# Router logits in two halves of 64 tokens, taken behind the values' products, and three smaller moves in a fused attention and expert kernel

## The chip, the core and the metric

The kernel is one launch on one core of a Trainium2 chip. The metric is the device time of that launch in microseconds (us), as the median of several runs. The profile names the engines: PE (TensorE, products), PEld (the loading of its weights, which overlaps PE), DVE (VectorE), ACT (ScalarE), POOL (GpSimd) and SP (SyncE, which here issues transfers).

## The reference, cut to what is computed

```python
def _attn_ref(q, k, v):                      # (4, 8, 576, 64) each
    scores = scale * np.matmul(q, k.transpose(0, 1, 3, 2))
    mask = (rel >= 0) & (rel < 64)           # a window of 64 keys
    ...
    attn = attn / (np.sum(attn, axis=-1, keepdims=True) + 1e-09)
    return np.matmul(attn, v)

def _moe_ref(x, w_gate, w_noise, noise, w1, w2):   # x (2304, 512), 8 experts, 1024 wide
    logits = x @ w_gate
    noise_scale = np.log1p(np.exp(x @ w_noise))
    noisy_logits = logits + noise_scale * noise
    top2 = np.argpartition(-noisy_logits, 2, axis=1)[:, :2]
    ...
    h = np.maximum(x[mask] @ w1[e], 0.0)
    out[mask] += top2_w[mask, k, None] * (h @ w2[e])

def _moe2_ref(x, w_in, w_out):               # 512 -> 2048 -> 512, a smooth gate between
    return g @ w_out
```

The output is `_moe2_ref(_moe_ref(_attn_ref(q, k, v)))`.

## The kernel before

**Stages.** The 2304 tokens are 18 tiles of 128. Attention and routing run first, up to about 103 us of the profile. Then the experts run in units: expert 0 as the units "0a" and "0b", experts 1 to 7, and last the wide layer. Everything is issued in the order in which the program writes it, engine by engine; no scheduler moves anything.

**The attention loop.** `step(u)` runs for u = 0 to 36, two steps for a tile. An even step u = 2m puts on PE, in this order: the masks and scores of tile m+1 (`A`, L355 and L364, products of 64 by 64), the turning of tile m-2's attention output (`Ex`, L422, four transposes), the turning of a block of probabilities (`C`, L387), and the values' products of tile m-1 (`Dm`, L401: 16 products, 32 on the chip since each fp32 product is two, with 64 weight columns; tokens 0 to 63 and 64 to 127 write different halves of the output partitions). The odd step has a second `C` and then the router's logits of tile m-2 (`Gm`, L440: four products with 128 weight columns and 16 moving columns, eight on the chip). Here one **turn** is the time from the `Ex` of one tile to the `Ex` of the next.

**The VectorE side of a turn.** Two reductions give the maxima of the scores (`top`, L371). `Dm` ends with the normalisation of tile m-1 (L406, L407, L409), which makes the tile `x` that the next turn's `Ex` reads. L443 copies the logits out of PSUM. Between them `advance` puts pieces of `route`, the routing of a group of tiles (8, 4 and 6 tiles): small operations on the logits and "marks", which are a row `ohr` by VectorE (L586) and a row `ohe` by VectorE (L593) or ScalarE (L596). `place` then gives each mark's product to PE (L634). When two groups are placed, `early` makes the first indexes and GpSimd gathers expert 0's rows.

**Banks.** The transposes of `C` and `Ex`, the logits and the routing counts take banks 3 and 5 in turn (`rot`). The values' products write the tile `OB`, two banks of which columns 0 to 259 are used. In unit "0b" (`WIDE - 1`) six blocks of the first full expert's rows are turned (`xpose`, L761): all in bank 7, and the sixth in bank 4. ScalarE copies each out (L767) and VectorE takes the difference (L768) before the next may write that bank.

**Loads.** SP loads keys and queries two tiles at a time (`load_qk`, L107 and L108), values, weights, and stores `x`.

## Time and profile before

| | us |
|---|---|
| median of 3 runs | 947.01 (946.17 to 947.58) |
| the profiled execution, whole | 950.02 |
| its span, first to last instruction | 948.3 |
| PE busy in the span | 935.7 |
| DVE, ACT, POOL busy | 665.6, 436.5, 186.2 |
| granted TensorE clock | 1.0 of full speed throughout |

PE is busy nearly all the time, but a pipelined engine that is shown busy need not be at its peak, and the share of busy time is a mean over stages. So the profile is read in stretches: busy time of each engine in each stretch, then the order of the instructions in a turn, then what ends the waits.

### The profile page before, as it was taken

The page shows a single profiled execution, that of the slowest core. Times are in us where ns is not written, and L with a number is a line of the kernel's source. Part 1 is how long each engine was busy: PE and PEld are TensorE (multiplying, and loading weights), DVE is VectorE, ACT ScalarE, POOL GpSimd, SP SyncE. Part 2 cuts the span into 40 slices and gives each one's busy share as a digit, 9 for nine tenths or more (in the row PEclk, how much of TensorE's full clock was granted, in tenths as well). Part 3 has the DMA queues.
Part 4 walks back from the last instruction along what each step waited for, and adds up shares of the span by engine and source line. Part 5 has one row for each costly group of instructions (what it writes and reads, how often), then busy time and mean ns, then how long its engine had stood idle before and what let it go on. Part 6 is the DMA issues. An engine that isn't in the chain of part 4 may idle for free. (4 is left out here: it accounts for less than half of the span.)

```text
span 948.3 us, 17990 instructions
## 1 busy us (share of the span) xinstructions
PE 935.7 (99%) x6779; PEld 832.3 (88%) x6781; DVE 665.6 (70%) x1411; ACT 436.5 (46%) x907; POOL 186.2 (20%) x249
## 2 busy tenths in 40 slices
PE   9999999999999999999999999999999999999998
PEld 6887888988888989898888889988999899899986
DVE  4689765477997968889533366767867776687664
ACT  6898314345565555555433266333433333342221
POOL 3222013133645353354402030000000000000000
PEclk9999999999999999999999999999999999999999
DMA  8874136555888878767725566775576559556521
GB/s 258 300 252 167 56 100 186 188 191 199 290 288 275 261 236 277 257 206 260 252 89 184 204 231 236 252 256 178 177 256 213 164 174 308 175 178 213 182 95 44
DMA packets 91274, 196.95 MB, mean 208 GB/s; under 512 B 7320, under 2 KB 18072, under 8 KB 91184
## 3 DMA queue, kind: packets, MB, share of 16 engines
q1 hardware_dynamic: 83152, 171.68, 54.6%
q0 software_dynamic: 6736, 21.86, 6.4%
q10 hardware_dynamic: 1296, 2.23, 0.6%
q8 instruction: 54, 0.88, 0.4%
q14 instruction: 36, 0.29, 0.1%
HBM read 155.45 MB, written 40.29 MB: 206 GB/s over the span
## 5 line engine op out<-in xcount | busy, mean ns | idle before, releaser
L969 PE MATMUL bank<-wo,hall 128*128 128x512 f32 x864 | 237.6, 394 | 0.0
L969 PE MATMUL bank<-w,hall 128*128 128x512 f32 (+3 forms) x944 | 234.6, 396 | 0.1
L969 PEld LDWEIGHTS bank<-w,hall 128*128 128x128 f32 (+3 forms) x944 | 167.7, 183 | 35.2 <-issue 0.3
L969 PEld LDWEIGHTS bank<-wo,hall 128*128 128x128 f32 x864 | 146.7, 188 | 17.4 <-DVE hall L915 0.2
L904 ACT ACTIVATE hall<-bank 128x288 fp32r<-128x288 f32 (+6 forms) x128 | 54.0, 422 | 218.4 <-PE bank L896 200.6
L896 PE MATMUL bank<-xhie,w 128*128 128x288 f32 (+4 forms) x768 | 122.5, 302 | 0.3 <-DVE hall L907 0.2
L896 PEld LDWEIGHTS bank<-xhie,w 128*128 128x128 f32 x768 | 113.5, 188 | 7.1 <-DVE hall L907 1.4
L907 DVE SCALAR_TENSOR_TENSOR hall<-bank,hall 128x288 fp32r<-128x288 f32 (+7 forms) x168 | 60.0, 391 | 82.5 <-ACT hall L904 75.1
L149 DVE TENSOR_TENSOR w<-raw,w 128x1024 fp32r<-128x1024 f32 (+1 forms) x69 | 81.9, 1188 | 23.8 <-ACT w L158 17.8
L1183 PEld LDWEIGHTS bank<-xb,wi 128*128 128x128 f32 x576 | 80.8, 188 | 8.4 <-DVE cg L1173 0.7
L1207 ACT ACTIVATE hall<-cg 128x512 fp32r<-128x512 f32 x64 | 40.3, 629 | 100.4 <-DVE cg L1205 100.4
L1183 PE MATMUL bank<-xb,wi 128*128 128x256 f32 x576 | 84.3, 282 | 0.3 <-DVE cg L1173 0.3
L1183 PEld LDWEIGHTS bank<-xc,wi 128*128 128x128 f32 x480 | 67.5, 188 | 6.5
L1183 PE MATMUL bank<-xc,wi 128*128 128x256 f32 x480 | 69.9, 280 | 0.0
L158 ACT ACTIVATE w<-raw 128x1024 fp32r<-128x1024 f32 (+1 forms) x71 | 69.4, 977 | 0.0
L896 PE MATMUL bank<-xloe,w 128*128 128x288 f32 (+4 forms) x384 | 69.0, 301 | 0.0
L1201 ACT ACTIVATE mg<-cg 128x512 f32<-128x512 f32 x64 | 40.1, 626 | 45.8 <-DVE cg L1173 44.1
L204 POOL TENSOR_TENSOR td<-rawd 128x512 f32<-128x512 f32 x32 | 33.3, 1040 | 139.6 <-DVE rawd L202 111.8
L896 PEld LDWEIGHTS bank<-xloe,w 128*128 128x128 f32 x384 | 58.0, 188 | 0.0
L1202 DVE SCALAR_TENSOR_TENSOR cg<-mg,cg 128x512 f32<-128x512 f32 x64 | 43.8, 684 | 18.8 <-ACT mg L1201 18.8
L1211 DVE SCALAR_TENSOR_TENSOR hall<-cg,hall 128x512 fp32r<-128x512 f32 x64 | 44.0, 687 | 8.1 <-ACT hall L1207 7.7
L1205 DVE SCALAR_TENSOR_TENSOR cg<-mg,cg 128x512 f32<-128x512 f32 x64 | 44.0, 687 | 1.0
(285 smaller groups left out, 1389.2 us busy)
## 6 DMA issues: line engine op xcount, KB each, us to landing
wi<-w1o SPq DMA_DIRECT2D x56, 1024.0 KB
raw<-wcat SPq DMA_DIRECT2D x64, 512.0 KB
rawd<-wd SPq DMA_DIRECT2D x32, 512.0 KB
w1o<-so SPq DMA_DIRECT2D x64, 256.0 KB
y<-y_dram SPq DMA_DIRECT2D x28, 256.0 KB
vE<-v SPq DMA_DIRECT2D x18, 260.0 KB
x_dram<-x SPq DMA_DIRECT2D x18, 256.0 KB
k<-kT SPq DMA_DIRECT2D x8, 512.0 KB
```

The lines of the kernel that those rows point to most:

```text
L149: nc.vector.tensor_tensor(out=w[:, 1, c], in0=t[:, c], in1=w[:, 0, c].bitcast(F32), op=ALU.subtract)
L158: nc.scalar.activation(w[:, 0, c], t[:, c], AF.Copy)
L896: nc.tensor.matmul(ps, lhsT=l[k], rhs=r[:, k, s:s + w], start=(c == 0), stop=(c == len(prods) - 1))
L904: nc.scalar.activation(hh, ps, AF.Relu)
L907: nc.vector.scalar_tensor_tensor(out=t, in0=ps[:, c], scalar=0.0, in1=hh[:, c].bitcast(F32), op0=ALU.max, op1=ALU.subtract)
L969: nc.tensor.matmul(M2[b][0:w], lhsT=h2[:, o:o + w], rhs=r[n], start=(first and a == 0), stop=(last and a == end))
L1183: nc.tensor.matmul(ps, lhsT=w[:, l, k * P:k * P + P], rhs=r[:, m, k, :], start=(c == 0), stop=(c == len(prods) - 1))
L1201: nc.scalar.activation(st["m"], c, AF.Relu, scale=0.5)
L1202: nc.vector.scalar_tensor_tensor(out=c, in0=st["m"], scalar=1.0, in1=c, op0=ALU.min, op1=ALU.subtract)
L1205: nc.vector.scalar_tensor_tensor(out=c, in0=st["m"], scalar=1.0, in1=c, op0=ALU.min, op1=ALU.mult)
L1207: nc.scalar.activation(h2[:, 0:T], c, AF.Copy, scale=-1.0)
L1211: nc.vector.scalar_tensor_tensor(out=h2[:, T:2 * T], in0=c, scalar=-1.0, in1=h2[:, 0:T].bitcast(F32), op0=ALU.mult, op1=ALU.subtract)
```

## The change

- **Logits.** `Gm` takes each 128-token tile as two halves of 64 tokens, so each product has 64 weight columns. It moves from the odd step to the even step, behind `Dm`, and writes columns 272 to 287 of `OB` in place of a bank of `rot`. `Dm` is now ahead of `early` and `advance`, and its normalisation is a function of its own, `norm`, that stays behind them.
- **Queries.** They are laid out tile by tile and half by half in DRAM, and loaded one tile at a time into four places.
- **Turned outputs.** For the first six tiles VectorE copies the turned output `xt`, between the two reductions; for the others ScalarE does, as before.
- **Banks.** The six transposes in unit "0b" take banks 7, 3, 5 and 4 in turn.

```diff
-    def load_qk(j):
-        q_t[j] = qbuf[:, j % 2]
+    def load_q(i):
+        nc.sync.dma_start(out=qbuf[:, i % 4], in_=qT[i])
+
+    def load_k(j):
         ...
             nc.sync.dma_start(out=kt[:, :, 64 + h.start:64 + h.stop], in_=kTv[:, :, t])
-            nc.sync.dma_start(out=q_t[j][:, :, h], in_=qTv[:, :, t])
+            if j < 2:
+                load_q(t.start // P)
+        if j == 1:
+            load_q(3)
...
+    def norm(u):
+        i, r = divmod(u, 2)
+        if r == 0:
+            return
         ov = OB[:, :, 0:4 * VW].rearrange("p b (h d) -> p b h d", d=VW)
...
-        nc.scalar.activation(xt.rearrange("p k t -> p (k t)"), XTb, AF.Copy)
         xts[i] = xt
+        if i < 6:
+            behind_top.append(lambda: nc.vector.tensor_copy(xt.rearrange("p k t -> p (k t)"), XTb))
+        else:
+            nc.scalar.activation(xt.rearrange("p k t -> p (k t)"), XTb, AF.Copy)
...
-        lg = (rot(u) if u <= NU else bank[0])[:, LGO:LGO + 2 * E]
+        lg = OB[:, i % 2, LGO:LGO + 2 * E]
         for k in range(4):
-            nc.tensor.matmul(lg, lhsT=xt[:, k, :], rhs=wg_sb[:, k, 0:2 * E], start=(k == 0), stop=(k == 3))
+            for h in (slice(0, 64), slice(64, P)):
+                nc.tensor.matmul(lg[h], lhsT=xt[:, k, h], rhs=wg_sb[:, k, 0:2 * E], start=(k == 0), stop=(k == 3))
...
             if (u + 2) % 4 == 0 and (u + 2) // 4 + 1 < NT // 2:
-                load_qk((u + 2) // 4 + 1)
+                load_k((u + 2) // 4 + 1)
                 keys_before((u + 2) // 4 + 1)
+            if u % 2 == 0 and u // 2 + 4 < NT:
+                load_q(u // 2 + 4)
...
             top(u + 2)
+            while behind_top:
+                behind_top.popleft()()
             top(u + 3)
         if u + 2 < NU:
             soft(u + 2)
 
-        if u % 2 == 1 and 0 <= m - 2 < NT:
+        place()
+        if 0 <= u - 1 < NU:
+            Dm(u - 1)
+        if u % 2 == 0 and 0 <= m - 2 < NT:
             logits(m - 2, u)
-        place()
         early()
         advance(MARKS[u > NU - 10])
         if 0 <= u - 1 < NU:
-            Dm(u - 1)
+            norm(u - 1)
...
     assert state["first"]
-    logits(NT - 2, NU)
     warm(2, Sb[0])
...
-                    prep_xpose(x, b, bank[0] if ui == WIDE else bank[4] if ui == WIDE - 1 and b == NB else TR)
+                    prep_xpose(x, b, bank[0] if ui == WIDE else bank[(7, 3, 5, 4)[b % 4]] if ui == WIDE - 1 else TR)
```

How the order moves at three places follows. In the rows `bank3_76` is bank 3 and so on, `p` are probabilities, `x13` is the output of tile 13, `xt13` the same turned.

PE before, in the turn of tile 13 (near 83 us of the profile), from the last values' product to the next masks:

```order
L401 MATMUL ob_106<-vE14_1429,pt29_1711 64x65
L387 MATMUL bank3_76<-idn_164,p31_1713 128x128 x4
L440 MATMUL bank5_77<-wg_sb_128,xt13_1778 128x16 x4
L558 LDWEIGHTS tri_172
L558 MATMUL bank3_76<-ohs1_1807,tri_172 128x32
...
L355 LDWEIGHTS id64_132
L355 MATMUL bank1_74<-mask00_134,id64_132 64x512
```

The same place after the change:

```order
L404 MATMUL ob_106<-vE14_1514,pt29_1796 64x65
L452 MATMUL ob_106<-wg_sb_129,xt13_1850 64x16 x8
L570 LDWEIGHTS tri_173
...
L390 MATMUL bank3_76<-idn_165,p31_1798 128x128 x4
L646 LDWEIGHTS ohr1_0_0_1914
L646 MATMUL bank7_78<-ohe1_0_0_1916,ohr1_0_0_1914 128x145
...
L358 LDWEIGHTS id64_133
L358 MATMUL bank1_74<-mask00_135,id64_133 64x512
```

The logits stand directly behind the values' products, as eight products of 64 columns in place of four of 128. The second block of probabilities is now followed by marks of the same turn (L646) and the masks, with no logits between.

DVE before, at the same place, from the two reductions to the next marks:

```order
L371 TENSOR_REDUCE mx33_1790<-bank0_73 128x4
L536 CAST ixf1_1803<-ix1_1728 128x8
...
L554 TENSOR_TENSOR Cn1_1811<-cs1_1809,Cn0_1400 128x8
L406 TENSOR_SCALAR rl14_1829<-ob_106 128x8
L407 RECIPROCAL rl14_1829<-rl14_1829 128x8
L409 TENSOR_TENSOR x14_1832<-ob_106,rl14_1829 128x512
L443 COPY lgs2_1722<-bank5_77 128x16
L567 TENSOR_TENSOR o21_1805<-o21_1805,bank3_76 128x64
```

The same place after:

```order
L374 TENSOR_REDUCE mx33_1862<-bank0_73 128x4
L455 COPY lgs2_1754<-ob_106 128x16
L579 TENSOR_TENSOR o21_1813<-o21_1813,bank5_77 128x64
...
L605 TENSOR_SCALAR ohe1_1_1_1928<-io145_180,rf1_1911 128x145
L414 TENSOR_SCALAR rl14_1930<-ob_106 128x8
L415 RECIPROCAL rl14_1930<-rl14_1930 128x8
L417 TENSOR_TENSOR x14_1933<-ob_106,rl14_1930 128x512
```

The copy of the logits and the routing work that followed the normalisation now stand ahead of it.

PE before, in unit "0b", the second block turned (`xge1_1`) and what stands around it:

```order
L896 MATMUL bank0_73<-xlo0b_2510,w4_1209 128x256 x4
L761 MATMUL bank7_78<-idr_170,xge1_1_2527 128x128 x4
L969 MATMUL bank2_75<-w3_1012,hall_2146 128x512 x3
L969 MATMUL bank6_2139<-w3_1012,hall_2146 128x512 x3
L896 MATMUL bank1_74<-xhi0b_2509,w5_1425 128x256 x8
```

After, the four blocks that follow the first:

```order
L779 MATMUL bank3_76<-idr_171,xge1_1_2607 128x128 x4
...
L779 MATMUL bank5_77<-idr_171,xge1_2_2681 128x128 x4
...
L779 MATMUL bank4_2218<-idr_171,xge1_3_2708 128x128 x4
...
L779 MATMUL bank7_78<-idr_171,xge1_4_2743 128x128 x4
L779 MATMUL bank3_76<-idr_171,xge1_5_2776 128x64 x4
```

The place of the transposes in the order is the same; their banks differ.

## Rows read from the trace of the kernel before

**Rows 1.** Page, part 1: busy time, share of the span, instructions.

```profile
PE 935.7 (99%) x6779; PEld 832.3 (88%) x6781; DVE 665.6 (70%) x1411; ACT 436.5 (46%) x907; POOL 186.2 (20%) x249
```

**Rows 2.** Busy time by stretch: us from the start, then each engine, clock, DMA.

```profile
20.00:62.60 42.60, 42.60 (x796) 37.97 (x795) 30.43 (x83) 38.98 (x113) 10.86 (x31) 1.00 0.82 276
62.60:85.00 22.40, 21.36 (x383) 18.41 (x382) 21.68 (x103) 19.47 (x60) 4.64 (x13) 1.00 0.71 235
85.00:103.70 18.70, 16.39 (x227) 13.38 (x224) 13.09 (x50) 10.15 (x27) 4.25 (x6) 1.00 0.37 115
150.00:155.00 5.00, 2.84 (x21) 2.49 (x20) 1.94 (x3) 2.54 (x5) 0.92 (x1) 1.00 0.62 189
155.00:175.00 20.00, 20.00 (x130) 18.67 (x129) 13.19 (x20) 9.77 (x17) 2.77 (x2) 1.00 0.55 170
300.00:400.00 100.00, 100.00 (x605) 89.78 (x604) 83.66 (x150) 53.77 (x104) 39.22 (x38) 1.00 0.77 256
```

**Rows 3.** One turn, weight loads of PE in time: start, us, instruction, idle before.

```profile
16.68 0.42 PEld L422 LDWEIGHTS bank<-idn,x 128*128 128x128 f32 x4 [0.17 <-issue]
17.07 0.47 PEld L387 LDWEIGHTS bank<-idn,p 128*128 128x128 f32 x4
17.70 1.01 PEld L401 LDWEIGHTS ob<-vE,pt 128*64 128x64 f32 x32 [0.17 <-issue]
18.79 0.42 PEld L387 LDWEIGHTS bank<-idn,p 128*128 128x128 f32 x4
19.18 0.97 PEld L440 LDWEIGHTS bank<-wg_sb,xt 128*128 128x128 f32 x8
20.18 0.11 PEld L355 LDWEIGHTS <-id 64*64 64x64 bf16 x4
...
21.39 0.20 PEld L422 LDWEIGHTS bank<-idn,x 128*128 128x128 f32 x2 [0.17 <-issue]
```

**Rows 4.** The same view where no logits stand between the block and the masks.

```profile
14.75 0.42 PEld L387 LDWEIGHTS bank<-idn,p 128*128 128x128 f32 x4
15.34 0.24 PEld L355 LDWEIGHTS <-id 64*64 64x64 bf16 x4 [0.17 <-issue]
```

**Rows 5.** Products on PE and normalisation on VectorE in time; ends of the second stretch.

```profile
22.41 1.15 PE L401 MATMUL ob<-vE,pt 128*64 128x65 f32 x32
23.50 0.66 PE L387 MATMUL bank<-idn,p 128*128 128x128 f32 x4
23.64 0.17 DVE L406 TENSOR_SCALAR rl<-ob 128x8 f32<-128x8 f32 x1 [0.76 <-PE ob L401]
...
49.70 0.66 PE L422 MATMUL bank<-idn,x 128*128 128x128 f32 x4
...
92.22 0.66 PE L422 MATMUL bank<-idn,x 128*128 128x128 f32 x4
```

**Rows 6.** VectorE in time, 82 to 92 us.

```profile
82.02 1.28 DVE L371 TENSOR_REDUCE mx<-bank 128x4 f32<-128x512 f32 x2
83.22 0.17 DVE L536 CAST ixf<-ix 128x8 f32<-128x8 uint32 x1
...
84.65 0.16 DVE L406 TENSOR_SCALAR rl<-ob 128x8 f32<-128x8 f32 x1
84.85 0.20 DVE L407 RECIPROCAL rl<-rl 128x8 f32<-128x8 f32 x1
85.08 0.69 DVE L409 TENSOR_TENSOR x<-ob,rl 128x512 f32<-128x512 f32 x1
85.69 0.16 DVE L443 COPY lgs<-bank 128x16 f32<-128x16 f32 x1
85.77 0.21 DVE L567 TENSOR_TENSOR o<-o,bank 128x64 f32<-128x64 f32 x1
...
90.58 0.30 DVE L586 TENSOR_SCALAR ohr<-io,rf,tcode 128x128 f16<-128x128 f16 x1
```

**Rows 7.** VectorE by stretch: copied logits to next reductions in eight turns.

```profile
53.79:54.27 0.48, 0.42 (x2) 1.00 1.06 373
58.16:59.07 0.91, 0.81 (x5) 1.00 0.35 115
63.13:64.23 1.10, 1.10 (x18) 1.00 1.09 254
68.16:69.89 1.73, 1.63 (x11) 1.00 0.78 194
73.57:75.00 1.43, 1.43 (x9) 1.00 1.03 369
79.98:82.02 2.04, 2.04 (x19) 1.00 0.54 152
85.77:88.13 2.36, 2.26 (x15) 1.00 0.62 182
92.09:93.40 1.31, 1.17 (x7) 1.00 0.35 133
```

**Rows 8.** ScalarE and PE in time: marks, and the last logits.

```profile
90.24 0.74 ACT L596 ACTIVATE ohe<-io,rf 128x145 f16<-128x145 f16 x2
90.82 0.56 PE L634 MATMUL bank<-ohe,ohr 128*128 128x145 f16 x4
...
101.46 1.06 PE L440 MATMUL bank<-wg_sb,xt 128*128 128x16 f32 x8 [0.45 <-ACT xt L424]
```

**Rows 9.** The wait in unit "0b": ACT, DVE and PE in time.

```profile
152.33 0.38 ACT L904 ACTIVATE hall<-bank 128x256 fp32r<-128x256 f32 x1 [4.44 <-PE bank L896]
152.61 0.59 ACT L767 ACTIVATE xhie<-bank 128x512 fp32r<-128x512 f32 x1
...
153.23 0.69 DVE L768 TENSOR_TENSOR xloe<-bank,xhie 128x512 fp32r<-128x512 f32 x1
...
153.98 0.54 PE L761 MATMUL bank<-idr,xge 128*128 128x128 f32 x4 [2.16 <-DVE xloe L768]
```

**Rows 10.** SP in time: one of the queries' ten loads.

```profile
21.92 0.50 SPq L108 DMA_DIRECT2D qbuf<-qT  x1
```

More of the change, by code (lines that the diff above doesn't have):

```diff
@@ L89, in fused_kernel @@
     kTv = kT.rearrange("(g p) t -> p g t", p=P)
-    qTv = qT.rearrange("(g p) t -> p g t", p=P)
     k_t, vE, vO = {}, {}, {}
@@ L95, in fused_kernel @@
     nc.vector.memset(wz, 0.0)
-    q_t = {}
-    qbuf = ring.tile([P, 2, 4, 256], F32, tag="w", name="qbuf")
-    def load_qk(j):
-        q_t[j] = qbuf[:, j % 2]
+    qbuf = ring.tile([P, 4, 2, 4, 64], F32, tag="w", name="qbuf")
+    def load_q(i):
+        nc.sync.dma_start(out=qbuf[:, i % 4], in_=qT[i])
+    def load_k(j):
         kt = k_t[j] = qk.tile([P, 4, 320], F32, tag="k", name=f"k{j}")
@@ L253, in fused_kernel @@
     nc.scalar.preload_act_table_set("natural_log_exp_and_others")
-    load_qk(0)
-    load_qk(1)
+    load_k(0)
+    load_k(1)
     load_v(0)
@@ L348, in A @@
         j = i // 2
-        qo, ko = (i % 2) * P, (i % 2) * P
+        ko = (i % 2) * P
         sb = [score(2 * i + k) for k in range(2)]
@@ L364, in A @@
                     nc.tensor.matmul(sb[k][64 * c:64 * c + 64, g * P:g * P + P],
-                                     lhsT=q_t[j][r, g, qo + 64 * c:qo + 64 * c + 64],
+                                     lhsT=qbuf[r, i % 4, c, g, :],
                                      rhs=keys, start=False, stop=(g == 3))
@@ L624, in bump @@
         yield 1
-    live, rows = [], {}
+    live, rows, behind_top = [], {}, deque()
     def place():
@@ L1481 @@
     f = np.ascontiguousarray
-    qT = f(q.transpose(1, 3, 0, 2).reshape(DM, N))
+    qT = f(q.transpose(1, 3, 0, 2).reshape(4, P, NT, 2, 64).transpose(2, 1, 3, 0, 4))
     kT = f(k.transpose(1, 3, 0, 2).reshape(DM, N))
```

## Prediction

> **What bounds the kernel now.** I read the page first: PE is busy 935.7 of 948.3 us [rows 1], so time is won only where PE's own work shrinks or a wait of PE goes. Then the stretches. From 20 to 62.6 us PE has no gap at all, while ScalarE is at 38.98 and VectorE at 30.43 of 42.60. From 62.6 to 85 us VectorE is the fullest engine (21.68 of 22.40) and PE begins to show gaps, and the end of attention has more. From 150 to 155 us PE is busy only 2.84 of 5.00; from 155 to 175 and in the later stretches it is full again, as the row of 300 to 400 shows [rows 2]. Last I read one turn of the attention loop in time, and what ends the wait at 152 us. So what the change wins at either place should reach the end: nothing behind it is waiting for anything but PE.
>
> The sum is made against the profiled execution, 950.02 us with 1.7 us outside its span. That is 3.0 us above the median of 947.01. I carry the difference, in us, over to the median.
>
> **First stretch, seven turns from 16.68 to 49.70 us.** A turn on PE is 0.39 us for the turned output, 0.63 for the first block of probabilities, 1.09 for the values' 32 products, 0.39 for the second block, 1.00 for the logits and 1.21 for masks and scores: 4.71 in all [rows 3]. The logits' eight products have 16 moving columns, but each takes 0.125 us, because of its 128 weight columns. After the change they are 16 products with 64 weight columns. The nearest row is the values' products, which have the same weight shape: 32 in 1.09 us [rows 3], so 16 in 0.54. This saves 0.46. Something comes back: where a block of probabilities is followed directly by the masks, the distance is 0.59 and not 0.39, with 0.17 of it shown as waiting for nothing [rows 4]. That costs 0.20. A turn becomes 4.71 - 1.00 + 0.54 + 0.20 = 4.45, a gain of 0.26, and seven turns give **-1.8 us**. The ends: -3.2 if the 0.20 is not paid (7 x 0.46), and +1.4 if the halves cost together what the whole did (7 x 0.20).
>
> [...] The row shows 32 loads of 64 columns, over the same 128 rows for both halves of the tokens, in 1.09 us, or 0.034 each, where a load of 128 columns with its product takes 0.125 [rows 3]: half of that would be 0.062, so the two halves overlap. [...]
>
> VectorE must keep pace. From the start of the turned output it is 0.39 + 0.63 + 1.09 = 2.11 to the end of the values' loads, 0.54 for the logits and 0.15 until VectorE begins (before, the normalisation begins 0.14 after PE goes on to the next block [rows 5]): 2.80. Copying the logits takes 0.1, the normalisation 1.12 until its last operation ends [rows 6], and 0.13 passes until PE has it: 4.15. That is under 4.45, so PE stays the bound here. The six copies of turned outputs on VectorE take 0.69 each by the normalisation's multiplication, which reads as many elements from PSUM [rows 6]. They stand between two reductions that take 1.2 together [rows 6]. The turned output ends on PE 0.66 into the turn [rows 5], so with 0.1 for the release the copy is done at about 1.5, before the logits start at 2.11. Without that cover they would cost 0.69 in each of six turns, 4.1 in all. ScalarE loses the same work; it was not the bound.
>
> **Second stretch, eight turns from 49.70 to 92.22 us.** They take 42.52 us [rows 5]. Here routing work joins. Before, VectorE does the normalisation as soon as the values are there, then copies the logits and does the routing pieces behind them. Now the copy, which waits for the logits on PE, and these pieces stand ahead of the normalisation, and behind it waits the turned output at the head of PE's queue, with everything that follows it on PE: probabilities, values, logits. The chain of a turn is 4.15 plus the routing pieces R. R is read before the change as the time from the copy to the next reductions: 0.48, 0.91, 1.10, 1.73, 1.43, 2.04, 2.36 and 1.31 [rows 7]. In the fifth the new order has two marks in place of four, so I take 1.43 - 2 x 0.30 = 0.8 [rows 6]. Their sum is 10.7. Twelve marks stand ahead of the values' products on PE, at 0.12 (four take 0.48 between starts [rows 8]): 1.4. So 8 x 4.15 + 10.7 + 1.4 = 45.3, which is **+2.8**. That is the low end. The high end: in four turns the marks of R are placed on PE ahead of the masks, so masks and scores also wait for R. From the end of R that path is 0.37 for a mark of ScalarE [rows 8], 0.12 and 0.17 on PE, and 1.21 for masks and scores [rows 3], 1.9 in all where the normalisation's path is 1.25. Four times 0.65 is 2.6, so +5.4. I take **+4.1**, halfway: ScalarE's marks need not wait for VectorE's, but they stand behind other work of ScalarE. The gain of 0.26 a turn is lost here, since PE is waiting.
>
> **End of attention.** The last logits take 1.06 on PE, and their end is waited for [rows 8]; as halves 0.54. I take **-0.5**, with ends 0 and -1.0 (the logits before them may shorten the path too).
>
> **Banks in unit "0b".** PE waits 2.16 us for the second block's turn, because VectorE's difference of the first block has not left bank 7. That stood behind ScalarE's copy, and this behind ScalarE's `hall` at 152.33 [rows 9]. With bank 3 the second block need not wait. But the products behind it need that same `hall`, which ends at 152.71: they started 0.37 after the transposes, so at 154.35, and could start at about 152.75. That is **-1.6**. Ends: -2.2 if `hall` comes earlier too, and 0 if the late `hall` is one of the things that make the profiled execution 3.0 us longer than the median.
>
> **What costs nothing.** The queries' loads go from 10 to 18. One holds SP for 0.50 us [rows 10]; eight more in 90 us delay values, weights and stores behind them by half a us each, and PE shows no wait for a load in these stretches. A tile's load waits until the scores of four tiles before have been made, one turn earlier; the loads of values and weights stand behind it. Without cover it is 0.5 us for each of 14. The store of `x` and GpSimd's copy of the values move with the normalisation, and both have a turn until anyone needs them.
>
> **Sum.** -1.8 + 4.1 - 0.5 - 1.6 = +0.2, so 947.0 + 0.2 = **947.2 us**. A measurement of this kernel can tell about 0.2% from no change, 1.9 us.
>
> **The rivals.**
> Faster: the marks do not hold the masks, so the second stretch costs its low end, +2.8, and the wait in "0b" goes whole, -2.2. With -1.8 and -1.0 at the end of attention that is -2.2: 944.8. For it: the path over the masks rests on ScalarE's marks, whose place in time no row shows for the new order. Against it: VectorE's own marks end with R, and PE has only the second block's 0.59 to do until then. Chance 0.25.
> Slower: the routing pieces ahead of the normalisation cost +5.4, and the late `hall` is not there in plain runs, so the banks give 0. -1.8 + 5.4 - 0.5 = +3.1: 950.1. It decides once the second stretch costs over 4.2 while the banks give nothing (-1.8 + 4.2 - 0.5 = 1.9). For it: VectorE was already the fullest engine there [rows 2]. Chance 0.22.
> The change does not do what it says: the halves do not overlap, each takes half of what the whole did, and the first stretch costs +1.4. [...] +1.4 + 4.1 - 0.5 - 1.6 = +3.4: 950.4. Against it stands the values' row. Chance 0.08.
>
> **How the numbers follow.** The forecast, no change that can be told, has 0.45; faster 0.25; slower 0.22 + 0.08 = 0.30. The range goes from every term at its good end, -3.2 + 2.8 - 1.0 - 2.2 = -3.6, to the last rival at +3.4: 943.4 to 950.4, which I take to leave out 2 in 10.
>
> **What the profile after would show.** First stretch: turned outputs 4.45 apart, and 16 products of the logits within 0.54 right behind the values. Second stretch: PE's turned output waiting for the normalisation, and the eight turns 45 to 48 us long. Unit "0b": no wait for VectorE's difference, at most half a us for `hall`. The prediction is wrong if VectorE's routing pieces turn out to lie beside PE's work, so that the second stretch is no longer than before (then it is faster), or if the turns of the first stretch do not shrink.

## The result, and the profile after

The changed kernel takes **958.87 us** (median of five runs, 957.79 to 960.47) where the kernel before, beside it on the same chip, takes 946.87 (946.17 to 947.58): a ratio of 1.0128, with a 95% interval of 1.0114 to 1.0143. It is slower; the forecast was 947.2 with a range up to 950.4.

The profiled executions differ by less: spans of 957.1 and 948.3 us, 8.8 apart. The one of before was itself 3 us above its median. When the changed kernel was measured again on another chip it took 958.79, and the kernel before beside it 950.66 (ratio 1.0092, 1.0074 to 1.0110). So 8 to 9 us are in the traces. In each of the four later comparisons, on four chips, the kernel before took 950.2 to 951.2, near its profiled execution; the other 3 us of the first comparison lie in its five runs of 946 to 948, of which no trace was kept, and they stay unexplained.

Page of the changed kernel, the row of part 1 and the clock of part 2:

```profile
PE 937.3 (98%) x6925; PEld 830.6 (87%) x6925; DVE 667.6 (70%) x1417; ACT 434.6 (45%) x901; POOL 185.6 (19%) x249
PEclk9999799999999999999999999999999999999999
```

The clock has a 7 in it, where PE's granted clock was 1.00 in every stretch shown of before [rows 2]. Three stretches of after (busy time of PE, PEld, DVE, ACT, POOL, then granted clock, DMA share, GB/s):

```profile
62.60:85.00 22.40, 18.89 (x318) 15.64 (x317) 18.50 (x84) 16.60 (x48) 3.62 (x11) 0.86 0.63 210
85.00:103.70 18.70, 13.20 (x227) 11.09 (x225) 9.08 (x42) 9.72 (x28) 5.06 (x8) 0.87 0.31 87
155.00:175.00 20.00, 20.00 (x136) 18.34 (x135) 13.69 (x18) 10.78 (x18) 3.91 (x5) 1.00 0.59 192
```

From 62.6 to 85 us PE is busy 18.89 where it was 21.36, and VectorE, the fullest engine there before with 21.68, has fallen to 18.50: they wait for each other. Unit "0b", whose wait stood at 152 us, now lies some 9 us later, in the last row: PE has no gap there. I cut the span where the prediction did, at the turned outputs of the attention loop, and at the first expert product:

| stretch | before | after | difference | predicted |
|---|---|---|---|---|
| start to first turned output | 16.68 | 17.01 | +0.33 | 0 |
| first stretch, seven turns | 33.02 | 30.68 | -2.34 | -1.8 |
| second stretch, eight turns | 42.52 | 49.14 | +6.62 | +4.1 |
| end of attention, to the first expert product | 11.51 | 16.37 | +4.86 | -0.5 |
| the rest | 844.57 | 843.90 | -0.67 | -1.6 |

These add to +8.8. In the rest, the 2.16 us of [rows 9] are gone and a new wait of 1.55 has come, told below under ScalarE's long store. What PE waited for in the changed kernel (line, releaser: us, times, longest):

```profile
PE bank L646 <- DVE ohr L598: 2.8, 2, 1.5
PE ob L404 <- POOL vE L423: 2.6, 1, 2.6
PE bank L430 <- DVE x L417: 1.9, 4, 0.9
```

L646 is the placing of marks, L404 the values' products, L423 GpSimd's copy of the values, L430 the turned output, L417 the end of the normalisation. In the second stretch alone PE waits 4.7 us for marks (L598, L605 and ScalarE's L608 together) and 0.6 us for the normalisation; the rest of the 1.9 lies at the end of attention.

**First stretch.** One turn, weight loads of PE in time, to be read beside [rows 3]:

```profile
34.66 0.42 PEld L430 LDWEIGHTS bank<-idn,x 128*128 128x128 f32 x4 [0.17 <-issue]
35.04 0.47 PEld L390 LDWEIGHTS bank<-idn,p 128*128 128x128 f32 x4
35.68 1.01 PEld L404 LDWEIGHTS ob<-vE,pt 128*64 128x64 f32 x32 [0.17 <-issue]
36.61 0.55 PEld L452 LDWEIGHTS ob<-wg_sb,xt 128*64 128x64 f32 x16
37.19 0.42 PEld L390 LDWEIGHTS bank<-idn,p 128*128 128x128 f32 x4
37.77 0.11 PEld L358 LDWEIGHTS <-id 64*64 64x64 bf16 x4 [0.17 <-issue]
...
38.99 0.20 PEld L430 LDWEIGHTS bank<-idn,x 128*128 128x128 f32 x2 [0.17 <-issue]
```

The turn is 4.33. The sixteen halves (L452) take 0.58 to the next block, the masks pay the 0.20 behind the block (37.19 to 37.77 is 0.58), and the values take 0.93 to the logits where they took 1.09 to a block: between these two groups of 64-column loads there is no gap (the values' end at 36.69, the logits' start at 36.61).

**Second stretch.** A turn of 7.15 us, PE and VectorE in time (L455 copies the logits, L579 to L598 are routing pieces, L417 is the end of the normalisation):

```profile
64.32 0.60 PE L452 MATMUL ob<-wg_sb,xt 128*64 128x16 f32 x16
65.16 0.16 DVE L455 COPY lgs<-ob 128x16 f32<-128x16 f32 x1
...
66.72 0.54 DVE L598 TENSOR_SCALAR ohr<-io,rf,tcode 128x128 f16<-128x128 f16 x2
67.26 0.53 PE L646 MATMUL bank<-ohe,ohr 128*128 128x145 f16 x2 [1.53 <-DVE ohr L598]
67.61 0.69 DVE L417 TENSOR_TENSOR x<-ob,rl 128x512 f32<-128x512 f32 x1
```

The pieces stand between the logits' copy and the normalisation, as the prediction said, and PE waits 1.53 us for a mark that is made of them; the normalisation, behind it, is not what PE waits for here. Then the clock falls. Stretches of 2 us (same columns as above):

```profile
66.00:68.00 2.00, 0.65 (x10) 0.40 (x14) 1.90 (x10) 1.40 (x5) 0.44 (x2) 1.00 0.16 63
68.00:70.00 2.00, 2.00 (x39) 1.67 (x32) 1.42 (x6) 2.00 (x7) 0.00 (x0) 0.58 0.38 134
...
80.00:82.00 2.00, 1.24 (x16) 0.62 (x19) 1.93 (x14) 2.00 (x7) 0.00 (x0) 0.99 0.04 14
82.00:84.00 2.00, 2.00 (x36) 1.67 (x27) 1.93 (x11) 0.95 (x3) 0.00 (x0) 0.50 0.37 134
...
98.00:100.00 2.00, 0.00 (x0) 0.00 (x0) 0.00 (x0) 0.09 (x1) 1.68 (x3) 0.76 0.70 236
100.00:102.00 2.00, 1.96 (x36) 1.96 (x38) 0.00 (x0) 0.00 (x0) 0.00 (x0) 0.50 0.78 236
```

PE was busy 0.65, 1.24 and 0.00 of 2 us, and behind each of these its granted clock was 0.50 to 0.58 in the mean: most or all of the next 2 us went at 0.50. In stretches of 0.2 us this trace shows 1.00 or 0.50, and a mean between them only where it changes.

**End of attention.** GpSimd and PE in time (L488 is the list that the gathers wait for, L752 the gathers):

```profile
95.13 0.16 DVE L488 SCALAR_TENSOR_TENSOR src_i<-few 128x3 int32<-128x3 f32 x1
95.59 1.23 POOL L752 DMA_INDIRECT xg0a<-x_dram,src_i  x1 [1.91 <-DVE src_i L488]
97.13 0.98 POOL L752 DMA_INDIRECT xg0a<-x_dram,src_i  x1 [0.30 <-issue]
98.42 0.94 POOL L752 DMA_INDIRECT xg0a<-x_dram,src_i  x1 [0.30 <-issue]
99.36 0.63 POOL L423 COPY vE<-vE 64x520 f32<-64x520 f32 x1
100.04 2.00 PE L404 MATMUL ob<-vE,pt 128*64 128x65 f32 x32 [2.58 <-POOL vE L423]
```

GpSimd's copy of the values stands behind three gathers, and these behind the list. Before, the copy ran at 89.80, 3.5 us ahead of the first gather:

```profile
89.80 0.65 POOL L415 COPY vE<-vE 64x520 f32<-64x520 f32 x1
93.34 1.24 POOL L734 DMA_INDIRECT xg0a<-x_dram,src_i  x1 [2.90 <-DVE src_i L476]
```

The 32 products of the values then take 2.00 us, at the lower clock (0.50), where they took 1.15 [rows 5]. So both a wait and the clock lengthen this stretch; the runs below take each away by itself.

### The profile page after: what moved, and what is told of

Read it like the earlier page. It is cut to its first block, busy times and chain, and to the rows that moved or that the text cites. A ratio compares the mean times of both kernels' runs of the same rounds, so it can differ in the third digit from the quotient of the medians.

```text
span 957.1 us, 18243 instructions
## 1 busy us (share of the span) xinstructions
PE 937.3 (98%) x6925; PEld 830.6 (87%) x6925; DVE 667.6 (70%) x1417; ACT 434.6 (45%) x901; POOL 185.6 (19%) x249
```

## The experiments

Theory A, formed on these two traces: moving the logits to the even step moved routing by half a step, so its pieces, marks and gathers now stand ahead of what PE waits for, and the waits bring PE's clock down. Rivals: another part of the change carries the loss (B), or the clock costs nothing because it lies in the shadow of the waits (A2). Stretches as in the table above; every ratio is to the kernel before on the same chip.

| run | us | ratio (95%) | first | second | end |
|---|---|---|---|---|---|
| changed kernel, again | 958.79 | 1.0092 (1.0074 to 1.0110) | 30.58 | 45.91 | 16.37 |
| norm_first | 986.39 | 1.0384 (1.0367 to 1.0401) | 40.75 | 60.65 | 18.92 |
| copy_first | 956.37 | 1.0061 (1.0044 to 1.0078) | 31.41 | 48.94 | 13.43 |
| logits_back | 948.32 | 0.9976 (0.9966 to 0.9985) | 32.94 | 42.51 | 11.41 |
| after_warm | 974.22 | 1.0258 (1.0241 to 1.0275) | 31.62 | 64.18 | 14.97 |
| norm_next | 962.31 | 1.0121 (1.0102 to 1.0139) | 30.60 | 51.63 | 13.50 |
| norm_next_even | 954.73 | 1.0036 (1.0024 to 1.0049) | 31.60 | 47.13 | 11.86 |
| marks_even | 956.80 | 1.0061 (1.0039 to 1.0082) | 31.56 | 46.96 | 14.70 |
| warm_rot | 954.92 | 1.0039 (1.0025 to 1.0053) | 30.83 | 46.23 | 13.51 |
| route_odd | 953.87 | 1.0030 (1.0018 to 1.0041) | 30.87 | 45.41 | 15.18 |
| route_odd_act4 | 955.12 | 1.0054 (1.0035 to 1.0073) | 31.38 | 45.84 | 14.30 |
| route_odd_whole | 959.33 | 1.0094 (1.0076 to 1.0111) | 34.05 | 49.11 | 13.06 |
| route_ahead | 948.54 | 0.9982 (0.9973 to 0.9991) | 31.97 | 41.97 | 12.83 |
| back_halves | 946.65 | 0.9967 (0.9954 to 0.9980) | 31.39 | 42.06 | 10.86 |
| after_act4 | 956.15 | 1.0058 (1.0042 to 1.0073) | 31.83 | 48.76 | 16.37 |

### Only the logits back (logits_back)

```diff
-        lg = OB[:, i % 2, LGO:LGO + 2 * E]
+        lg = (rot(u) if u <= NU else bank[0])[:, LGO:LGO + 2 * E]
...
-        if u % 2 == 0 and 0 <= m - 2 < NT:
-            logits(m - 2, u)
...
+        if u % 2 == 1 and 0 <= m - 2 < NT:
+            logits(m - 2, u)
         place()
```

The products are whole again and the values' products stand behind the routing pieces again, which the lines shown leave out.

> The changed kernel with the logits as they were: eight whole products in the odd step, into the rotating bank. The queries' loads, VectorE's six copies and the four banks stay. Theory A (the logits' new place alone carries the loss, the other edits cost nothing and the banks give 2.2): 944 to 945.5 us, turns of 4.71 in the first stretch, clock 1.00. Theory B (VectorE's copies or the queries' loads carry part of the loss): 948 us or more, with a longer second stretch.

The ratio is 0.9976, 1.9 us under the kernel before beside it (950.26). The time of 948.32 by itself would fall to theory B; but both theories were set against the 946.87 of the first comparison, and against the kernel before theory A's 944 to 945.5 is 1.4 to 2.9 us under, which is what came. First and second stretch are 32.94 and 42.51 where they were 33.02 and 42.52, the clock is 1.00. So queries' loads and VectorE's copies cost nothing here, the banks give about what was read for them (the rest, behind attention, is 1.7 us shorter than before), and the move of the logits, with what moved along with it, is the whole loss. B falls.

### The normalisation first (norm_first)

```diff
             Dm(u - 1)
+            norm(u - 1)
         if u % 2 == 0 and 0 <= m - 2 < NT:
             logits(m - 2, u)
         early()
         advance(MARKS[u > NU - 10])
-        if 0 <= u - 1 < NU:
-            norm(u - 1)
```

> The changed kernel with the normalisation (and the store of x and GpSimd's copy of the values that go with it) directly behind the values' products, ahead of the logits' copy, the routing pieces and the gathers. Theory A (the loss of 11.9 us comes from what now stands ahead of the normalisation on VectorE and of the copy on GpSimd, and from the clock that falls in the waits that follow): the second stretch returns to 42 to 43 us from 49.1, the end of attention to about 11 us from 16.4, the granted clock to 1.00. The first stretch keeps its 4.33 a turn and the banks their 2.2: 942 to 944 us, which is faster than the kernel before. Theory B (VectorE's six extra copies, the smaller loads of the queries or the logits' new bank carry the loss): the order of the normalisation matters little, 950 us or more.

Both theories missed: 986 us, turns of 5.81 in the first stretch. What PE waited for:

```profile
PE ob L452 <- DVE x L417: 24.4, 17, 3.2
```

The logits go into the output's banks. Written behind the normalisation, they wait until it has read them. So as long as the logits are written into the output's banks they must stand ahead of the normalisation; the run doesn't test theory A.

### GpSimd's copy ahead of the gathers (copy_first)

```diff
     def Dm(u):
...
+        if i + 1 < NT:
+            if i + 2 < NT:
+                nc.gpsimd.tensor_copy(vE[i][0:64, :], vE[i + 1][0:64, :])
+            vO[i + 1] = vE[i]
     def norm(u):
...
-        if i + 1 < NT:
-            if i + 2 < NT:
-                nc.gpsimd.tensor_copy(vE[i][0:64, :], vE[i + 1][0:64, :])
-            vO[i + 1] = vE[i]
```

> The changed kernel with GpSimd's copy of the values alone put back directly behind the values' products, so that it stands ahead of the three gathers; VectorE's normalisation stays where the change put it. [...] The second stretch stays at about 49 us. Theory B (the end is late because the routing pieces ahead of the gathers are late, the copy is only the last to be named): 957 to 959 us.

The wait for the copy is gone, the end of attention falls from 16.37 to 13.43, the time from 958.8 to 956.4, and the second stretch stays (48.94). So theory A, here that PE waits for the copy behind the gathers, holds for 2.9 us of the 4.86, with a time a little over the 953 to 955 it was put at. The clock still falls, now at 102.5 us, behind another wait of PE (2.3 us, for the normalisation, whose turn comes late; see the last paragraph of this document), but for a shorter time. The end of attention in the changed kernel and in copy_first (columns as above):

```profile
96.83:113.20 16.37, 12.39 (x147) 9.96 (x147) 4.97 (x17) 4.16 (x8) 2.55 (x3) 0.69 0.33 98
97.42:110.85 13.43, 10.16 (x147) 8.26 (x147) 4.88 (x17) 4.17 (x8) 1.93 (x3) 0.87 0.40 119
```

The mean clock rises from 0.69 to 0.87, so the 2.9 us hold some of the clock's price beside the wait for the copy.

### PE kept busy in its waits (after_warm, warm_rot)

```diff
+        if u > 20 and u % 2 == 1:
+            warm(16, OB[:, 1, 384:512])
+        if u == NU - 2:
+            warm(40, OB[:, 1, 384:512])
         place()
```

> The changed kernel with PE kept busy in its waits of the second stretch: 16 products of zeros with 128 columns in every odd step from u = 21 on, ahead of the marks, and 40 more in step 34, where PE waits for GpSimd's copy; their results go to columns of the output bank that nobody reads. The chain of waits is otherwise unchanged. [...] Theory A2 (the lower clock lies in the shadow of VectorE's chain): the clock stays at 1.00, but the time is 958 to 961 us, since the added products cost about what they give.

The run missed its aim in the same way as norm_first, since the added products go into the output's bank:

```profile
PE ob L668 <- DVE x L417: 17.0, 8, 3.1
```

In warm_rot they go into `bank[3 + 2 * ((turn[0] + 1) % 2)][:, 0:P]`, a bank that has been read by then.

> The changed kernel with PE kept busy in its waits of the second stretch by products of zeros (16 with 128 columns ahead of the marks in every odd step from u = 21, 40 more in step 34), this time into a bank of the turned outputs that has been read, since those into the output's banks waited for the normalisation (17.0 us in eight turns). [...]

The time is 954.92, 3.9 us under the changed kernel by the medians and 5 by the ratios, although 168 products were added. All runs show a clock of 0.999 or 1.000, where those of the changed kernel show 0.990 to 0.995. From 62.6 to 85 us and the end of attention in warm_rot, then from 62.6 to 85 us in the changed kernel measured again:

```profile
62.60:85.00 22.40, 21.37 (x438) 18.52 (x431) 19.39 (x86) 18.31 (x53) 4.38 (x13) 1.00 0.63 218
94.19:107.71 13.52, 11.64 (x203) 10.10 (x204) 4.89 (x17) 4.16 (x8) 2.55 (x3) 1.00 0.38 118
```

```profile
62.60:85.00 22.40, 18.60 (x378) 15.45 (x376) 19.51 (x88) 18.34 (x53) 4.40 (x13) 1.00 0.62 213
```

A2 falls: the run is 3.7 us over the kernel before, where A2 was put at 11 to 13. A1, that PE's work at the lower clock behind its waits is a good part of the loss, was put at 6 to 9; but it stood on 12 us for the changed kernel, and against the 8.1 of its second measurement (next section) the gain of 4 to 5 us is within the 3 to 6 that A1 meant. In the profiled executions the gain lies at the end: 13.51 us for 16.37, with GpSimd's copy still behind the gathers, while the second stretch was at a clock of 1.00 in both.

### The changed kernel again (after_again)

> The changed kernel itself, on the same chip as the runs beside it, as their measure. Both theories: 11 to 13 us over the kernel before, second stretch 49 us, end of attention 16 us, ScalarE's long store near 620 us.

It is 8.1 us over the kernel before, not 11 to 13, and the second stretch of this execution is 45.91 us, not 49. The same code with the same waits of PE (2.8 us for L598's marks and 2.6 for GpSimd's copy in both); but here the clock was 1.00 up to 85 us (row above) and fell only at the end. From 66 to 68 us PE was busy 0.60 of 2 us, less than in the other execution, and the clock stayed. The two executions price the clock in the second stretch by themselves: 49.14 - 45.91 = 3.2 us. At the end both have a mean clock of 0.69 and the same 16.37 us.

### The normalisation between logits and routing (norm_next, norm_next_even, marks_even)

```diff
             logits(m - 2, u)
+        if 0 <= u - 1 < NU:
+            norm(u - 1)
         early()
         advance(MARKS[u > NU - 10])
-        if 0 <= u - 1 < NU:
-            norm(u - 1)
```

> The changed kernel with the normalisation (with the store of x and GpSimd's copy) behind the logits' copy but ahead of the routing pieces and of the gathers. The logits' products, which share the output's banks, then no longer wait for the normalisation, as they did in the run that put it ahead of them (24.4 us of waits in 17 turns). Theory A (routing pieces and gathers ahead of the normalisation carry the loss): second stretch 42 to 43 us, end of attention about 11.5 us, 3 to 5 us faster than the kernel before. Theory C (the marks, which PE now takes ahead of the masks, carry a good part: in four turns masks and scores wait for normalisation, routing pieces and marks together, 5.9 us plus the pieces): second stretch 46 to 48 us, time 1 to 4 us over the kernel before.

It is no better than the changed kernel: 51.63 us in the second stretch, worse than either theory gave. PE now waits 8.8 us for the marks (5.7 and 3.1), since the pieces that make them stand behind the normalisation and the masks behind the marks. norm_next_even adds, and marks_even makes alone, this edit:

```diff
-        place()
+        if u % 2 == 0:
+            place()
```

> The run before this one in the list, and the marks placed in even steps alone, so that PE takes them behind masks, turned output and probabilities, as the kernel before did for most of them. Theories A and C agree here: second stretch 42 to 43 us, end of attention about 11.5, clock 1.00, turns of 4.33 in the first stretch: 3 to 5 us faster than the kernel before. Theory D (VectorE is full in that stretch, and with the logits half a turn earlier nothing can be won or kept there): no faster than the run with the logits back in their old place, 2 us below the kernel before.

> The changed kernel with the marks placed in even steps alone; the normalisation stays behind the routing pieces and the gathers. Theory A: the normalisation's path is the longer one, so little changes: 10 to 13 us over the kernel before, second stretch 48 to 50 us. Theory C (masks that wait for the marks, and PE's clock that falls in that wait at 66 to 67 us, carry part): second stretch 45 to 47 us, 7 to 10 us over the kernel before, and no fall of the clock at 68 us. The end of attention stays near 16 us in both.

With both, 954.73: better than the changed kernel, but the second stretch is 47.13, not 42 to 43, so the forecast that A and C shared failed. With the marks alone, 956.80: 2 us under the changed kernel as measured again and 5.6 over the kernel before, better than either theory gave, with a second stretch in C's range. The clock is 1.00 from 62.6 to 85 us, as C had it, but 0.83 in the mean from there to the end of the second stretch, so the 46.96 can't be set against the 45.91 of the changed kernel, which has no such fall. PE no longer waits for marks in that stretch, but for the normalisation, where the changed kernel waited 0.6 us for it:

```profile
PE bank L430 <- DVE x L417: 4.7, 5, 1.9
```

The two paths are nearly as long, and this run does not show a cost of the marks' place beyond the clock. In norm_next_even PE places a whole step's marks right ahead of the values, and waits for ScalarE's copies of probabilities (2.6 us) that stand behind ScalarE's marks. Changing one queue's order moves the wait to the next.

### Routing put off by half a step (route_odd, route_odd_whole, route_ahead)

```diff
-            live.append(route(g))
-            next(live[-1])
+            begun.append(g)
...
+        if u % 2:
+            begin()
         place()
```

> The changed kernel with the start of routing for a group of tiles put off from the even step, where the group's last logits now stand, to the odd step behind it. The routing pieces, the marks, and the gathers with them, then fall into the same steps as in the kernel before, while logits as halves behind the values, queries' loads, VectorE's copies and banks stay as changed. Theory E (the loss comes from the half step by which routing moved: its long pieces stand ahead of the normalisation, its marks ahead of masks or values, its gathers ahead of GpSimd's copy; the clock falls in the waits that this makes): second stretch 42 to 43.5 us, end of attention 11 to 12, clock 1.00, 2 to 5 us faster than the kernel before. Theory D (VectorE is full there and the logits' copy in the even step costs by itself): second stretch 45 us or more, slower than the kernel before.

Theory E failed: 45.41 us in the second stretch, 3.2 us over the kernel before, as theory D of this run had it. The marks' waits are smaller, but VectorE, the fullest engine of this stretch, waits in the middle of its queue (route_odd, VectorE in time):

```profile
83.84 0.17 DVE L455 COPY lgs<-ob 128x16 f32<-128x16 f32 x1 [0.64 <-PE ob L452]
```

VectorE's wait in the whole second stretch (us, times, longest):

```profile
DVE lgs L455 <- PE ob L452: 5.4, 7, 1.2
```

It waits for the logits, with a routing piece behind the copy (L548, at 83.93) that was ready. route_ahead changes that and keeps the rest:

```diff
         place()
+        early()
+        advance(MARKS[u > NU - 10])
         if 0 <= u - 1 < NU:
             Dm(u - 1)
         if u % 2 == 0 and 0 <= m - 2 < NT:
             logits(m - 2, u)
-        early()
-        advance(MARKS[u > NU - 10])
```

> The changed kernel with the start of routing put off to the odd step, and in every step the routing pieces and marks ahead of the values, logits and normalisation on VectorE, as they stood in the kernel before; the logits' copy then has only the normalisation behind it. Theory D (in the run with the routing put off, VectorE waited 0.6 to 0.9 us in most turns for the logits it had to copy, with pieces queued behind that it could have done; this wait is what is left of the second stretch's loss): second stretch 42.5 to 43.5 us, turns of 4.33 in the first, 1 to 4 us faster than the kernel before. Theory H (the marks' place on PE ahead of the masks is what is left): second stretch stays at 45 us or more, slower than the kernel before.

The second stretch is 41.97 us and the ratio 0.9982. The same place in time:

```profile
81.86 0.16 DVE L548 CAST ixf<-ix 128x8 f32<-128x8 uint32 x1
83.31 0.17 DVE L455 COPY lgs<-ob 128x16 f32<-128x16 f32 x1
83.39 0.16 DVE L414 TENSOR_SCALAR rl<-ob 128x8 f32<-128x8 f32 x1
```

The pieces run ahead, the copy waits for nothing here (1.2 us once in the whole stretch), and the normalisation follows. Theory D as it stands for this run, that VectorE's waits were what was left, holds, and H falls: the marks stand on PE as in route_odd.

route_odd_whole is route_odd with eight products of 128 tokens (`nc.tensor.matmul(lg, lhsT=xt[:, k, :], ...)`).

> The first run of this list with the logits as eight products of 128 tokens in place of sixteen of 64. If the halves overlap, as the turns of 4.33 us say, the whole ones cost 0.46 more in every turn of the first stretch: turns of 4.79 us, 3 us more there, 2 to 4 us more in the time. If the gain of the turn comes from the new place of the logits and not from the halves: turns of 4.3 to 4.5 us and the same time within 1 us.

Turns of 4.79 and 4.80, a first stretch 3.2 us longer. The halves save the 0.46 a turn that was read for them. The time is 5.5 us longer, more than expected, since the second stretch also grew.

### The halves in the old place (back_halves)

The edit is to logits_back.

```diff
-            nc.tensor.matmul(lg, lhsT=xt[:, k, :], rhs=wg_sb[:, k, 0:2 * E], start=(k == 0), stop=(k == 3))
+            for h in (slice(0, 64), slice(64, P)):
+                nc.tensor.matmul(lg[h], lhsT=xt[:, k, h], rhs=wg_sb[:, k, 0:2 * E], start=(k == 0), stop=(k == 3))
```

> The run with the logits in their old step and bank, as sixteen products of 64 tokens in place of eight of 128; queries' loads, VectorE's copies and banks stay as changed. If the halves carry the whole gain of the first stretch (0.54 for 1.00, measured in the changed kernel as 0.53 from the first half's load to the next block): turns of 4.71 - 0.46 = 4.25 us, 3.2 us less there, the second stretch as before (VectorE is full there), and with the banks' 2.2: 4 to 6 us faster than the kernel before. If ScalarE or VectorE bounds the turn at less than that: turns of 4.3 to 4.7 us, 2 to 4 us faster.

**946.65 us, 0.9967 (0.9954 to 0.9980): it beats both kernels**, 3.6 us under the one before. The gain is under the 4 to 6 of the first forecast: the turn is 4.48, not 4.25. Turn and time lie in the second forecast's ranges, but neither ScalarE nor VectorE is the cause. The weight loads show why:

```profile
40.31 0.42 PEld L390 LDWEIGHTS bank<-idn,p 128*128 128x128 f32 x4
40.90 0.55 PEld L452 LDWEIGHTS bank<-wg_sb,xt 128*64 128x64 f32 x16 [0.17 <-issue]
41.47 0.11 PEld L358 LDWEIGHTS <-id 64*64 64x64 bf16 x4
```

Here the logits pay the gap behind a block of 128 columns (0.59), which the whole ones did not (0.39 [rows 3]). Against logits_back, the same kernel with whole products, the first stretch is 1.6 us shorter in the traces; the two ratios (0.9954 to 0.9980 and 0.9966 to 0.9985) overlap, so in the whole time the halves' gain here is not clear of the noise.

### ScalarE's long store (route_odd_act4, after_act4)

```diff
+    nop = ac.tile([P, 1], F32, name="nop")
+    for _ in range(4):
+        nc.scalar.activation(nop, wz[:, 0:1], AF.Copy)
     def step(u):
```

> The run before this one in the list with four tiny ScalarE instructions (one column each) ahead of the attention loop; nothing else changes. In every run with the logits in the even step ScalarE's first store of an output tile, near 616 to 648 us, held ScalarE for 2.6 to 3.1 us (0.4 in the kernel before and with the logits back), PE waited 1.4 to 1.9 us behind it, and a packet of the queue that carries instructions landed within it; that store was instruction 964 in ScalarE's program, where it is 968 with the logits back and 978 in the kernel before. Theory F (the wait is ScalarE's code arriving at that place of its program): shifted by four the store takes 0.4 us and PE's wait goes, 1.5 us off the time. Theory G (the wait has to do with the traffic at that time): it stays, and the time is the same.

route_odd had the short store already (0.38), so this pair told nothing. It was made again on the changed kernel.

> The changed kernel with four tiny ScalarE instructions ahead of the attention loop. ScalarE's first store of an output tile moves from instruction 964 of its program to 968. In the runs so far the store was long where it was number 964 and short where it was 965, 968, 969 or 978. Theory F (ScalarE waits there for its code): the store takes 0.4 us, PE's wait of 1.4 to 1.9 us goes, about 1.5 us off the 958.8 of the changed kernel. Theory G (the other differences of those kernels made it short): 2.6 us or more, the same time.

The store and PE's wait behind it in the changed kernel, what the queue of instructions moved from 621.4 to 622.2 us (packets, MB, share), and the store with the four instructions ahead:

```profile
620.42 2.69 ACTq L1009 DMA_DIRECT2D out<-yg  x1
...
624.12 0.98 PE L1200 MATMUL bank<-xb,wi 128*128 128x256 f32 x6 [1.55 <-ACT sg L1181]
```

```profile
q14 instruction: 1, 0.01, 2.4%
```

```profile
623.55 0.38 ACTq L1013 DMA_DIRECT2D out<-yg  x1
```

Theory F's forecast holds: 0.38, PE's wait is gone, 956.15 us. That is 2.6 us under the changed kernel measured again, more than the 1.5 of the wait; the rest may be noise, since route_odd_act4, whose store was short with and without the four instructions, came out 1.2 us over route_odd. Counted in the traces' records of ScalarE, the store is number 914 in the nine traces where it is long and 915, 918, 919 or 928 in the eight where it is short (the expectations count 50 more for each). In all nine one 8 KB packet of the queue of instructions lands during the long store; in the other eight none lands near it. That ScalarE waits for its code is argued from these two facts, and no trace shows the wait by that name.

## Why the prediction was wrong, point by point

**First stretch: right, and a little better.** -2.34 for -1.8. The halves overlap, the gap behind the block is paid (0.58 for 0.39). Missed was the 0.16 that falls away where the logits follow the values, so 4.33 for 4.45. One of the seven turns took 4.65. Halves that do not overlap, the prediction's last rival, would have given turns of 4.9; the trace has 16 loads over the same rows in 0.55 us.

**VectorE's copies and the queries' loads: right for the copies, a little short for the loads.** logits_back shows both free at turns of 4.71. In several runs with turns of 4.33 PE waited for a load once or twice inside the attention loop, in most of them for keys (0.2 to 1.3 us, at 29 to 56 us) and in two for queries (0.5 in marks_even, 1.2 in route_ahead), and in after_again and after_act4 for the first queries ahead of it (0.9 and 1.6); the kernel before, logits_back and back_halves show no such wait. The prediction had "PE shows no wait for a load in these stretches" from the slower turns.

**Second stretch: the order of the work was right, and a resource was missing.** Without the fall of the clock it takes 45.91 us (after_again) or 46.23 (warm_rot), +3.4 and +3.7 for +4.1. With it 49.14. The step that failed is "The chain of a turn is 4.15 plus the routing pieces R": it prices every PE part of the chain, and of the masks' path, from rows at a clock of 1.00, and the lower level, 0.50, cost 3.2 us here. The prediction found that PE would wait, and did not ask what PE does behind a wait. The longest wait of PE in this stretch before is 0.3 us, so no row of before showed the lower level. The 0.13 us in the 4.15, from the normalisation's end to PE, was the author's estimate without a row; the changed kernel's trace shows 0.05 to 0.14 there.

The sum's size at a clock of 1.00 was near, but in part by luck. It is built on PE waiting for the normalisation, with the masks' wait for the marks as an addition of at most 2.6; measured, PE waited 4.7 us for marks and 0.6 for the normalisation. The two paths are nearly as long, as marks_even shows, and so the wrong one gave a fair total.

**End of attention: wrong in sign, +4.86 for -0.5.** The step that failed is the sentence that the store of `x` "and GpSimd's copy of the values move with the normalisation, and both have a turn until anyone needs them". In most turns this is so. In the one turn where the gathers are issued, the copy moved past three of them (1.23, 0.98, 0.94 us) and past the list that they wait for. The order of GpSimd's queue told this before the run; the prediction had named the move and had not followed it to the one step where something long stands in between. With the copy ahead of the gathers (copy_first) the end is 2.9 us shorter. With the copy left where it was and the clock held at 1.00 (warm_rot) it is 2.9 shorter too. The first of these also raises the mean clock, so the two shares overlap, and no run takes them apart. The sum had neither.

**Banks: right.** The wait of 2.16 us went whole, where 1.6 was taken because `hall` would be late; in the changed kernel `hall` was not waited for there.

**The rest: a wait of 1.55 us that nothing in the prediction could have given**, from where ScalarE's store fell in its program.

**The sum.** 0.33 - 2.34 + 6.62 + 4.86 - 2.16 + 1.55 = +8.9, against +0.2. The clock has about 3.2 of it in the second stretch; at the end, the copy behind the gathers and the clock have up to 2.9 each. The chance of 0.30 for slower was too small, and the range ended at 950.4 because both rivals on that side were made from the same terms at their other ends: neither had a new wait or a slower PE in it.

## What to carry to other kernels

When work moves between the steps of a loop, follow each of its queues to the one step where that queue also carries something long, because "a turn until anyone needs it" is an average over steps. Where a change makes PE wait on a stretch in which it did not wait before, price what PE does next at both granted clocks that these traces show, 1.00 and 0.50. A half that pays off can be taken without the move that came with it: the kernel with the lowest median here keeps the old order and takes the smaller products, with the changed loads, copies and banks.

## What the runs showed of the hardware

**The clock.** The granted clock fell to 0.50 behind stretches in which PE had been busy 0.65 or 1.24 of 2 us, in an engine busy 98% of the span, and not in each execution: at 68 us in one, only at the end in the other, where PE had been busy 0.60 of 2 us at the same place. Products of zeros in those waits kept it at 1.00 and were worth 3.9 us net.

**ScalarE's long store.** One place in the program goes with it: a store took 2.6 to 3.1 us as number 914 of ScalarE's records and 0.38 as 915, 918, 919 or 928, and a packet of the queue that carries instructions landed during each long one. In the changed kernel the long store (2.69 us) stood on PE's path with 1.55 us.

**Gaps between weight widths.** 0.17 us, shown as waiting for nothing, stand ahead of loads of 64 columns that follow loads of 128, as at 35.68, 37.77 and 40.90, and ahead of the turned output's 128 columns behind the scores' 64 columns of 64 rows, as at 38.99. At 37.19, where a block of 128 columns follows the logits' 64 columns of 128 rows, there is no such gap (0.03). What makes the gap, no run shows.

**Late answers beside the gathers, left open.** While GpSimd issued the gathers, VectorE and ScalarE saw PE's products late. In route_odd:

```profile
94.47 0.60 PE L452 MATMUL ob<-wg_sb,xt 128*64 128x16 f32 x16
...
96.78 0.95 POOL L760 DMA_INDIRECT xg0a<-x_dram,src_i  x1 [0.30 <-issue]
...
98.36 0.17 DVE L455 COPY lgs<-ob 128x16 f32<-128x16 f32 x1 [4.34 <-remote]
```

The logits' end is modelled at 95.07, and their copy, which waits for them alone, starts 3.3 us later, 0.6 after the last gather's record ends; in copy_first the same distance is 1.1. ScalarE's copy of the turned probabilities (L392) starts at 98.51, 2.8 us after the modelled end of their product at 95.67. PE's next turned output waits 4.0 us in route_odd, for the normalisation behind this copy. Whether PE ended later than its records say, or its signal was held up, these runs don't tell, and no run was made to take the gathers away.
